# Pooled attention and a two-layer mixer on one core: one group of scores one slot later, two transposes swapped, fifteen idle products instead of sixteen

## The chip, the core and the metric

The kernel runs on one core of a Trainium2 chip. The core has a matrix engine (TensorE, PE in the profile, with its weight loads shown as PEld), a vector engine (VectorE, DVE), an activation engine (ScalarE, ACT), a general engine (GpSimd, POOL) and a queue engine that issues transfers (SyncE, SP); ACT and POOL issue transfers as well. Each engine takes its instructions in a fixed order and waits at semaphores for the others. The metric is the time of one execution on the device in microseconds (us), the median of several runs.

## The reference

Batch 8, 8 heads, 576 tokens, head size 64. Keys and values are averaged over 8 neighbouring tokens, so that each head has 72 of them.

```python
k_p = k.reshape(B, H, Sp, pool, D).mean(axis=3)
v_p = v.reshape(B, H, Sp, pool, D).mean(axis=3)
scores = scale * np.matmul(q, k_p.transpose(0, 1, 3, 2))
scores = scores - np.max(scores, axis=-1, keepdims=True)
attn = np.exp(scores)
attn = attn / (np.sum(attn, axis=-1, keepdims=True) + 1e-09)
attn_out = np.matmul(attn, v_p).astype(np.float32)
...
x = np.ascontiguousarray(attn_out.transpose(0, 2, 1, 3)).reshape(B, S, H * D)
a1 = alpha1 * x + beta1
tok = np.einsum('ts,bsd->btd', w_tok, a1)
u = x + lam * tok
a2 = alpha2 * u + beta2
ch = np.maximum(a2 @ w_ch1, 0.0) @ w_ch2
return (u + lam * ch).astype(np.float32)
```

So there are three stages for each batch: attention over the pooled keys, a mix over the tokens (`w_tok`, 576 x 576), and a two-layer network over the channels (512 to 2048 to 512).

## The kernel before

**Chunks and blocks.** The tokens of a batch are held as four chunks of 128 rows and a rest of 64; the rests of two batches make one more chunk, called (b, 4) by the even batch. Four chunks make a block of 512 rows, and there are nine blocks, n = 0 to 8. The channel network runs block by block. Chunks go in the order (0,0) to (0,3), (1,0) to (1,3), (0,4), (2,0) and so on, so that the second block (n = 1) is the four chunks of batch 1, and its fourth chunk is (1,3).

**The order is written by hand.** Everything ahead of the first block stands in a string of names (from L1116), where each name advances one small generator. From then on, each block n builds a list of pairs (slot, action), sorts it by slot and runs it: that order is the program order on all engines at once, and each engine keeps its own instructions in it. A slot is one unit of matrix work of the block. In block n also the attention of batch n + 1 is done (`attention(b)`, b = n + 1), along with the loads for batch n + 2. The lines of the actions that matter here:

- `mlp_A` (L930, activation L938): one hidden slice j of 16, four products of 128x512 into a bank of the pool psA, then a ReLU by ACT. In block 0, slices 12 to 15 stand in slots 12 to 15.
- `mlp_B` (L951): four products of the second layer for chunk m; `finish_B` (L960, L961) adds the result to the output on DVE in block 0 and issues the store (L970) on SP.
- `att_S4` (L740 for the main rows, L747 for the last 64 rows): the scores of four heads. They take two banks of the pool psB ("lo"), two of psA ("hi") and two more of psA for the last 64 rows ("r"). Six exponentials (L769, ACT) read them: first the two r banks, then pair after pair of the others.
- `att_AV` (L784, L788, then DVE L791 and L793): attention times values of one head, and the division. `att_X` (L807, L800) multiplies two heads' result by a vector into xs, on POOL or DVE; `mix_T` (L873, then DVE L880 and a cast on ACT, L884) is the token mix of a chunk.
- `mix_uT` (L893): transposes a mixed chunk into u_fm, the moving operand of `mlp_A` of its block; from the second block on it is a transposing transfer issued by SP. `att_F` (L586) does the same for the q rows of a batch (qT), and `att_Frem` (L612) for its last 64 rows (rem_qT), which `cast_rem` (L351) has cast on POOL.
- `keep_warm` (L862): products on a tile of zeros that no one reads, ahead of the first real work; two more are issued by "wa" in the string.
- `scale_w2` (L982): multiplies a piece of the second layer's weights by lam, on DVE or POOL; `sum_k` (L360, L362, POOL) sums neighbouring key rows; `att_V` (L692, DVE) does so for values.

Pool psA has six banks and psB two. A bank is handed out again once its last tile's readers, in program order, have been issued; the first instruction that writes it waits for them.

In block 0, with b = 1, the scores of heads 0 to 3 stand in slot 9.0 and those of heads 4 to 7 in slot 12.9; the exponentials, the AVs of heads 4 to 7 and their att_X stand at fixed distances behind them. The transposes of chunks (1,0) to (1,3) stand in slots 23.8, 24.9, 26.0 and 27.1, the one of (0,4) in 28.2, and `att_Frem(2)` in 26.22.

Of the kernel before, what the change touches and what calls it, by code (L numbers as in the profile page):

```python
# [210 lines left out]
def kernel(  # L211
# [30 lines left out]
    def gp(name):  # L242
        if pair[0]:
            return psB.tile([P, 512], FP, tag="ch", bufs=2, name=name)
        return psA.tile([P, 512], FP, tag="gp", name=name)

    def whole(parts):
        for _ in parts:
            pass
# [13 lines left out]
    def new_batch(b):  # L263
        st1[b] = {"qT": [None] * 2, "ET": [None] * H, "raw": [None] * 2, "q": [None] * 2,
                  "k": [None] * 2, "v": [None] * 2}
# [192 lines left out]
    def which_part():  # L458

        one = identity_bf[0:12, 0:12]  # L460
        four = const.tile([12, 4], FP, tag="four", name="four")
        nc.vector.tensor_reduce(out=four, in_=one.rearrange("p (k c) -> p c k", c=4), op=ALU.add,
                                axis=AX.X)
        nc.vector.tensor_copy(out=pick, in_=four.unsqueeze(2).to_broadcast((12, 4, P)))
        for i in range(2):
            nc.vector.tensor_reduce(out=less[:, i:i + 1], in_=one[:, 4 + 4 * i:], op=ALU.add,
                                    axis=AX.X)
        nc.vector.tensor_scalar(out=less, in0=less, scalar1=-1.0, scalar2=None, op0=ALU.mult)
# [108 lines left out]
    def att_F(b, hp, copy=nc.scalar.copy):  # L577


        st = st1[b]  # L580
        u, r = hp // 2, hp % 2
        if st["qT"][u] is None:
            st["qT"][u] = work.tile([P, 8, P], BF, tag="qT", bufs=4, name="qT")
        if b > 1:
            if r == 0:
                nc.sync.dma_start_transpose(out=st["qT"][u],  # L586
                                            in_=st["q"][u].rearrange("p h c d -> p (h c d)"))
            return
        ps_q = gp("ps_q").bitcast(BF)
        for c in range(4):  # L590
            nc.tensor.transpose(
                out=ps_q[:, 128 * c:128 * c + 128],
                in_=st["q"][u][:, 2 * r + c // 2, 2 * (c % 2):2 * (c % 2) + 2].rearrange(
                    "p c d -> p (c d)"),
                identity=identity_bf)

        yield
        copy(out=st["qT"][u][:, 4 * r:4 * r + 4, :],
             in_=ps_q[:, 0:512].rearrange("p (c t) -> p c t", c=4))

    def att_Frem(b, copy=None):

        st = st1[b]
        if b > 2:
            rem = room()[:, 2048:2560].rearrange("p (c t) -> p c t", c=4)
            st["rem_qT"], st["rem_kT"] = rem[:, 0:2], rem[:, 2:4]
            nc.sync.dma_start_transpose(out=rem,
                                        in_=st["rem_both"].rearrange("p c h d -> p (c h d)"))
            return
        st["rem_qT"] = work.tile([P, 2, P], BF, tag="rem_qT", bufs=2, name="rem_qT")  # L610
        if copy is None:
            nc.sync.dma_start_transpose(out=st["rem_qT"],  # L612
                                        in_=st["rem"][0].rearrange("p c h d -> p (c h d)"))
            return
        ps_q = gp("ps_qr").bitcast(BF)
        for c in range(2):
            nc.tensor.transpose(out=ps_q[:, 128 * c:128 * c + 128],
                                in_=st["rem"][0][:, c].rearrange("p h d -> p (h d)"),
                                identity=identity_bf)
        yield  # L620
        copy(out=st["rem_qT"], in_=ps_q[:, 0:256].rearrange("p (c t) -> p c t", c=2))
# [8 lines left out]
    def room():  # L630
        if "room" not in late:
            late["room"] = const.tile([P, 2560], BF, tag="wt_bf", name="late_room")
        return late["room"]
# [224 lines left out]
    def keep_warm(count, ps=None):  # L858

        ps = ps or psB.tile([P, DM], FP, tag="ch", bufs=2, name="ps_warm")  # L860
        for _ in range(count):
            nc.tensor.matmul(out=ps, lhsT=warm[:, 0:P], rhs=warm)  # L862
        return ps
# [202 lines left out]


    new_batch(1)
    warmed = keep_warm(16)
    which_part()  # L1070
    more_constants()

# [56 lines left out]
    def attention(b):  # L1129


        first = b == 1
        todo = []
        if first:
            for hp in range(4):
                todo.append((2.6 + 0.9 * hp, lambda hp=hp: whole(att_F(b, hp))))
            todo.append((3.5, lambda: cast_rem(b, nc.gpsimd, behind=nc.vector)))
            for u in range(2):
                todo.append((3.65 + 0.1 * u, lambda u=u: load_w2(2 + u)))
            todo.append((7.4, lambda: whole(att_Frem(b, nc.scalar.copy))))  # L1140
        if b < B - 1:
            at = 28.5 if first else 10.0
            todo.append((at, lambda: whole(att_F(b + 1, 0))))
            todo.append((at + 0.1, lambda: whole(att_F(b + 1, 2))))
            todo.append((19.3 if first else 23.1, lambda: cast_rem(
                b + 1, nc.gpsimd, behind=None if first else nc.vector)))
            todo.append((26.72 if b > 1 else 26.22, lambda: whole(att_Frem(b + 1))))
        for u in range(2):
            if first:
                todo.append((3.6 + 0.1 * u, lambda u=u: sum_k(b, u, nc.gpsimd)))  # L1150
            if 1 < b < B - 1:
                todo.append((26.5 + 0.1 * u, lambda u=u: sum_k(b + 1, u, nc.gpsimd)))
                todo.append((26.73 + 0.1 * u, lambda u=u: turn_k(b + 1, u)))
            if b > 2:
                todo.append((4.1 + 2.0 * u, lambda u=u: pool_k(b, u)))
                continue
            if first:
                todo.append((19.1 + 0.1 * u, lambda u=u: sum_k(2, u, nc.gpsimd)))
            todo.append((7.0 + 2.3 * u if first else 2.9 + 2.0 * u,
                         lambda u=u: whole(  # L1160
                             att_K(b, u, nc.vector.tensor_copy if first else nc.scalar.copy))))
        for u in range(2):
            at = (9.0, 12.9)[u] if first else (6.3, 13.6)[u]
            todo.append((at, lambda u=u: att_S4(b, u)))
            for k, dt in enumerate((0.1, 0.1, 0.1, 0.7, 1.7, 1.75) if u else (0.1, 0.1, 0.1, 1.1, 2.1, 3.1)):
                todo.append((at + dt, lambda u=u, k=k: st1[b]["exp", u](k)))
            early = (5.2, 5.7, 3.7, 4.2) if first else (5.7, 6.2, 2.9, 3.4)
            for i, dt in enumerate((2.9, 3.4, 4.6, 5.1) if u else early):
                h = 4 * u + i
                todo.append((at + dt, lambda h=h: whole(att_AV(b, h))))  # L1170
                if i % 2:
                    eng = nc.gpsimd if h == 5 or first and h < 5 else nc.vector
                    todo.append((at + dt + 0.1, lambda h=h, eng=eng: att_X(b, h - 1, h + 1, eng)))
        for u in range(2):
            when = (0.2, 1.4, 2.2), (10.0, 12.8, 13.0) if b == 2 else (5.0, 7.2, 8.0)
            if first:
                when = (10.6, 10.7, 10.8), (12.5, 12.6, 12.7)
            for i, at in enumerate(when[u]):
                todo.append((at, lambda u=u, i=i: att_V(b, u, 4 >> i)))
        for c in range(5):  # L1180
            at = 22.0 + 1.1 * c if first else 21.0 + (1.3 if b == 2 else 1.15) * c
            if c < 4 or b % 2:
                todo.append((at, lambda c=c: whole(mix_T(b, c))))
                key = (b, c) if c < 4 else (b - 1, 4)
                todo.append((at + 1.8, lambda key=key: whole(mix_uT(key))))
        return todo

    for n in range(NBLK):
        todo = []
        for j in range(0 if n else 4, NJ):  # L1190
# [3 lines left out]
            else:  # L1194
                at = 8 * (j // 4 % 2) + 4 * (j // 8) + j % 4 if n >= FIRST else j
                todo.append((at, lambda j=j: whole(mlp_A(n, j))))
        for m in range(4 if n < FIRST else 0):
            for part in range(4):
                at = 16 + (4 * part + m if n == 0 else 2 * part + (m if m < 2 else 6 + m))
# [56 lines left out]
        b = n + 1  # L1256
        if b < B:
            todo += attention(b)
            if b + 1 < B:
                new_batch(b + 1)  # L1260
                gate = nc.vector if b == 1 else None
                for u in range(2):
                    at = (15.31 if b == 1 else 21.0) + 0.01 * u
                    todo.append((at, lambda b=b, u=u: load_k(b + 1, u, gate)))
                    at = {1: 14.0, 2: 6.5}.get(b, 0.4) + 0.1 * u
                    todo.append((at, lambda b=b, u=u: load_q_bf(
                        b + 1, u, nc.vector if b == 2 else None)))
                    at = 15.35 + 0.01 * u if b == 1 else ((6.7, 13.2) if b == 2 else (3.5, 7.5))[u]
# [42 lines left out]
```

## Time and profile before

| | us |
|---|---|
| median of three runs | 330.04 (329.70 to 330.65) |
| the profiled execution | 331.23 |
| its span, first to last instruction | 329.4 |
| PE busy | 320.9 |
| DVE, ACT, POOL busy | 236.0, 175.6, 115.8 |
| first idle products to first transposes (PE) | 1.51 to 8.09 |
| first block of the channel network, from its first slice on PE to the start of the second block | 25.15 to 67.55 |
| second block | 67.55 to 102.88 |

The span is what lies between the first and the last instruction; the execution's time has some 1.8 us around it. The granted clock of PE is 1.00 throughout. A row of the timeline gives start, duration, engine, line, operation and the tiles written and read; in brackets at its end stands the idle time ahead of it on its engine, and the instruction whose end the profile holds to have released it. SPq and POOLq rows are the issue of a transfer, not the transfer itself.

### The profile page before, as it was taken

To read this page: it belongs to the slowest core of one execution; us is meant where nothing else is said; L and a number is where in the kernel's file an instruction comes from. 1 tells how busy PE (TensorE), PEld (TensorE's weight loads), DVE (VectorE), ACT (ScalarE), POOL (GpSimd) and SP (SyncE) were. 2 spreads that over 40 slices of the span, in tenths; PEclk is the share of its full clock that TensorE was granted. 3 is DMA by queue.
4 is the path that set the end of the run, shared out by engine and by line. 5 is a ranking of instruction groups with operands and counts; after the bars stand their busy time and mean duration, and the time that the engine had idled before them with its cause. 6 is when DMAs were issued, how large, how long until landed. Compare 5 with 4: busy or idle time off the path is not lost.

```text
span 329.4 us, 6466 instructions
## 1 busy us (share of the span) xinstructions
PE 320.9 (97%) x2473; PEld 206.4 (63%) x2473; DVE 236.0 (72%) x494; ACT 175.6 (53%) x326; POOL 115.8 (35%) x140
## 2 busy tenths in 40 slices
PE   8999989999999999999999999999999999999995
PEld 3689644445544576656775577558755866586584
DVE  6783576996689979786967787887788793263263
ACT  3868979258433951387128803782368235803710
POOL 8687354996246010800280027102510560000000
PEclk9999999999999999999999999999999999999999
DMA  7999979988896893499549943996480025003013
GB/s 197 204 231 254 214 149 265 142 165 170 174 254 103 211 191 90 75 265 178 155 87 242 188 147 81 164 230 180 100 178 0 2 54 158 0 2 127 0 34 96
DMA packets 73351, 47.40 MB, mean 144 GB/s; under 512 B 41283, under 2 KB 64099, under 8 KB 73319
## 3 DMA queue, kind: packets, MB, share of 16 engines
q1 hardware_dynamic: 59302, 34.78, 45.7%
q0 software_dynamic: 12896, 11.28, 21.5%
q10 hardware_dynamic: 1120, 0.92, 0.9%
q8 instruction: 19, 0.31, 0.4%
q14 instruction: 14, 0.11, 0.1%
HBM read 38.31 MB, written 9.44 MB: 145 GB/s over the span
## 4 chain that ended last, share of the span: by engine, by line
PE 82%; DMA 5%; DVE 4%; POOL 3%; issue 3%; ACT 1%; POOLq 0%; SPq 0%; DVEq 0%; ACTq 0%
PE ps_h L930 34%; PE ps_w L1047 23%; PE ps_tok L873 10%; PE ps_ch L951 7%; DMA v<-in_v_dram 2%; DMA kT<-k_bf 2%; PE ps_s L740 2%; PE ps_av L784 2%; ACT H L938 1%; POOL k_bf L362 1%; DVE x_tm L793 1%; POOL k_raw L360 1%; DVE w L982 1%; PE ps_r L747 1%; PE ps_w L516 1%
## 5 line engine op out<-in xcount | busy, mean ns | idle before, releaser
L930 PE MATMUL ps_h<-u_fm,w 128*128 128x512 bf16 (+2 forms) x608 | 132.8, 369 | 2.0 <-DVE u_sb L961 0.8
L938 ACT ACTIVATE H<-ps_h,bias_cols 128x512 bf16<-128x512 f32 x144 | 98.3, 689 | 56.8 <-PE ps_h L930 55.4
L930 PEld LDWEIGHTS <-w 128*128 128x128 bf16 x608 | 65.7, 114 | 53.0 <-issue 4.4
L1047 PEld LDWEIGHTS <-H 128*128 128x128 bf16 x560 | 53.5, 98 | 10.8 <-DVE u_sb L1065 1.2
L884 ACT CAST u_bf<-u_sb 128x512 bf16<-128x512 f32 x34 | 21.1, 619 | 71.3 <-issue 41.4
L1047 PE MATMUL ps_w<-w,H 128*128 128x256 bf16 x448 | 53.6, 273 | 0.0
L807 POOL TENSOR_TENSOR xs<-x_tm,lamal_bc 128x512 bf16<-128x512 f32 x12 | 15.2, 1270 | 104.2 <-DVE x_tm L793 104.0
L1065 DVE TENSOR_TENSOR u_sb<-u_sb,ps_w 128x512 f32<-128x512 f32 x54 | 36.3, 684 | 17.5 <-PE ps_w L1047 17.0
L873 PE MATMUL ps_tok<-xs,wtT 128*128 128x512 bf16 (+5 forms) x220 | 45.1, 361 | 0.0
L880 DVE TENSOR_TENSOR u_sb<-x_tm,ps_tok 128x512 f32<-128x512 f32 (+1 forms) x40 | 27.2, 683 | 8.9 <-PE ps_tok L873 8.9
L793 DVE TENSOR_TENSOR x_tm<-ps_av,recs 128x320 f32<-128x320 f32 x64 | 31.4, 491 | 2.7
L769 ACT ACTIVATE ET<-ps_s 72x512 f16<-72x512 f32 x56 | 32.3, 593 | 0.0
L951 PE MATMUL ps_ch<-w,H 128*128 128x512 bf16 x128 | 30.4, 379 | 0.0
L873 PEld LDWEIGHTS <-wtT 128*128 128x128 bf16 (+3 forms) x220 | 19.2, 100 | 15.2 <-issue 1.1
L791 DVE RECIPROCAL recs<-ps_av 128x5 f32<-128x5 f32 x64 | 12.0, 188 | 18.3 <-PE ps_av L788 18.0
L692 DVE TENSOR_TENSOR v_u<-v_u 72x1024 f32<-72x1024 f32 (+1 forms) x24 | 24.5, 1021 | 0.2
L1047 PE MATMUL ps_w<-w_t,h_s 128*128 128x256 bf16 x168 | 22.6, 272 | 0.0
L360 POOL TENSOR_TENSOR k_raw<-k_raw 128x512 f32<-128x512 f32 x14 | 19.2, 1369 | 4.5 <-DMA k_raw<-in_k_dram 4.5
L951 PEld LDWEIGHTS <-H 128*128 128x128 bf16 x128 | 11.9, 98 | 13.7 <-issue 0.4
L362 POOL TENSOR_TENSOR k_bf<-k_raw 128x512 bf16<-128x512 f32 x14 | 19.1, 1366 | 1.1
L1016 DVE TENSOR_TENSOR h_s<-H 128x1024 bf16<-128x1024 bf16 x21 | 14.6, 696 | 6.3 <-ACT H L938 5.8
L1047 PEld LDWEIGHTS <-h_s 128*128 128x128 bf16 x168 | 16.4, 98 | 4.1
(161 smaller groups left out, 349.8 us busy)
## 6 DMA issues: line engine op xcount, KB each, us to landing
out_dram<-u_sb SPq DMA_DIRECT2D x29, 256.0 KB, 4.1
k_raw<-in_k_dram SPq DMA_DIRECT2D x13, 512.0 KB, 5.7
v_u<-in_v_dram SPq DMA_DIRECT2D x12, 512.0 KB, 5.8
q_bf<-in_q_dram POOLq DMA_DIRECT2D x15, 256.0 KB, 5.6
w<-in_moe_w_ch_dram POOLq DMA_DIRECT2D x6, 512.0 KB, 14.0
out_dram<-u_sb SPq DMA_DIRECT2D x11, 128.0 KB, 2.4
v<-in_v_dram POOLq DMA_DIRECT2D x4, 288.0 KB, 10.4
w<-in_moe_w_ch_dram POOLq DMA_DIRECT2D x1, 1024.0 KB, 14.1
```

Of the source, the lines that this page charges most:

```text
L360: eng.tensor_tensor(out=raw[:, :, 0:2], in0=raw[:, :, 0:2], in1=raw[:, :, 2:4], op=ALU.add)
L362: eng.tensor_tensor(out=bf, in0=twice[0], in1=twice[1], op=ALU.add)
L692: nc.vector.tensor_tensor(out=out, in0=source[:, :, 0:width], in1=source[:, :, width:2 * width], op=ALU.add)
L769: nc.scalar.activation(out=o, in_=i, func=AF.Exp, bias=0.0, scale=0.125 if b < 3 else 0.125 * 0.125)
L793: nc.vector.tensor_tensor(out=x[:, 1 - odd:6 - odd, dd:dd + D], in0=av[:, :, 0:64], in1=rec.unsqueeze(2).to_broadcast((P, 5, D)), op=ALU.mult)
L873: nc.tensor.matmul(out=ps_tok[p0:p1, cols], lhsT=wtT[0:kk, at, P * c:P * c + p1 - p0], rhs=xs_pool[i][0:kk, sc, cols], start=(sc == 0), st ...
L880: nc.vector.tensor_tensor(out=s["u"][p0:p1, :], in0=x[p0:p1, 1 + c if c < 4 else 5 - 5 * i, :], in1=ps_tok[p0:p1, 0:DM], op=ALU.add)
L930: nc.tensor.matmul(out=ps_h[:, t0:t1 + one], lhsT=w1_of(cc, j), rhs=rhs, start=(cc == 0), stop=(cc == 3))
L938: nc.scalar.activation(out=H4[n, j // 4][:, j % 4, :], in_=ps_h, func=AF.Relu, bias=bias_cols[:, j:j + 1], scale=1.0)
L951: nc.tensor.matmul(out=ps, lhsT=H_of(n, j)[:, 128 * m:128 * m + 128], rhs=w2[j // 4][:, j % 4, :], start=(j == 0), stop=(j == NJ - 1))
L1047: nc.tensor.matmul(out=ps, lhsT=stat(j), rhs=moving(j), stop=(j == 7), start=(first and (pp == 0 or alone) and j == 0), skip_group_check=True)
L1065: nc.vector.tensor_tensor(out=o, in0=o, in1=banks[key, "both"], op=ALU.add)
```

## The change

Three numbers change.

```diff
     new_batch(1)
-    warmed = keep_warm(16)
+    warmed = keep_warm(15)
     which_part()
...
-            todo.append((26.72 if b > 1 else 26.22, lambda: whole(att_Frem(b + 1))))
+            todo.append((26.72 if b > 1 else 27.2, lambda: whole(att_Frem(b + 1))))
...
         for u in range(2):
-            at = (9.0, 12.9)[u] if first else (6.3, 13.6)[u]
+            at = (9.0 if first else 6.3, 13.6)[u]
             todo.append((at, lambda u=u: att_S4(b, u)))
             for k, dt in enumerate((0.1, 0.1, 0.1, 0.7, 1.7, 1.75) if u else (0.1, 0.1, 0.1, 1.1, 2.1, 3.1)):
                 todo.append((at + dt, lambda u=u, k=k: st1[b]["exp", u](k)))
```

Sorted by slot, block 0 then has these sequences (all else keeps its place):

```
before: slice 12, AV 2, scores 4-7, slice 13, exp 0 1 2, AV 3, X 2-3, exp 3, slice 14, AV 0, exp 4 5, AV 1, X 0-1, slice 15, loads,
        AV 4, B0, AV 5, X 4-5, B1, AV 6, B2, AV 7, X 6-7, B3
after:  slice 12, AV 2, slice 13, AV 3, X 2-3, scores 4-7, exp 0 1 2, slice 14, AV 0, exp 3, AV 1, X 0-1, slice 15, exp 4, loads (exp 5 among them),
        B0, AV 4, B1, AV 5, X 4-5, B2, AV 6, AV 7, X 6-7, B3
...
before: transpose (1,2), q rows of batch 2 (last 64), mix (0,4), B2, transpose (1,3), B0, finish, transpose (0,4), qT of batch 2
after:  transpose (1,2), mix (0,4), B2, transpose (1,3), q rows of batch 2 (last 64), B0, finish, transpose (0,4), qT of batch 2
```

Here "exp" are the exponentials of heads 4 to 7, B0 to B3 the second layer's products of chunks 0 to 3, and "loads" those for batch 2. In the other batches nothing changes: the two slots for b > 1 are the same in both versions.

## The prediction

> **What bounds the kernel now.** I read part 1 of the page first, then the list of waits over the whole span.
>
> ```profile
> span 329.4 us, 6466 instructions
> PE 320.9 (97%) x2473; PEld 206.4 (63%) x2473; DVE 236.0 (72%) x494; ACT 175.6 (53%) x326; POOL 115.8 (35%) x140
> ```
> ```profile
> PE ps_warm L862 <- DVE early L402: 1.5, 1, 1.5
> PE ps_s L740 <- ACT ET L769: 0.9, 1, 0.9
> PE ps_h L930 <- DVE u_sb L961: 0.8, 1, 0.8
> PE ps_h L930 <- ACT H L938: 0.6, 1, 0.6
> PE ps_sc L702 <- ACT kp L671: 0.5, 1, 0.5
> ```
> TensorE (PE) is idle for 8.5 us, of which 3.35 us lie behind its last work (326.05 to 329.4) and 1.5 us ahead of its first. So the kernel is a list of matmuls with few holes, and only a hole that closes, without another opening, makes it shorter. The 0.9, the 0.6 and the 0.8 lie in or right behind the first block, where the change works. The timelines of these places, all engines, come next (columns: start, duration).
>
> ```profile
> 40.49 0.28 PE L784 MATMUL ps_av<-vp,ET 72*128 72x66 f16 x4
> 40.73 0.30 PE L740 MATMUL ps_s<-qT,kp 64*72 64x256 bf16 x1
> 41.34 0.58 ACT L769 ACTIVATE ET<-ps_s 72x512 f16<-72x512 f32 x1
> 41.97 0.27 PE L740 MATMUL ps_s<-qT,kp 64*72 64x256 bf16 x1 [0.94 <-ACT ET L769]
> 42.37 0.49 DVE L793 TENSOR_TENSOR x_tm<-ps_av,recs 128x320 f32<-128x320 f32 x1
> 42.66 1.06 PE L930 MATMUL ps_h<-u_fm,w 128*128 128x512 bf16 x4
> 43.75 0.69 ACT L938 ACTIVATE H<-ps_h,bias_cols 128x512 bf16<-128x512 f32 x1 [1.83 <-PE ps_h L930]
> 44.49 1.03 PE L930 MATMUL ps_h<-u_fm,w 128*128 128x512 bf16 x4 [0.62 <-ACT H L938]
> ```
> ```profile
> 61.02 0.62 ACT L884 CAST u_bf<-u_sb 128x512 bf16<-128x512 f32 x1 [1.32 <-DVE u_sb L880]
> 63.69 1.17 SPq L612 DMA_TRANSPOSE rem_qT<-rem_q  x1
> 64.95 1.22 SPq L893 DMA_TRANSPOSE u_fm<-u_bf  x1
> 66.80 0.69 DVE L961 TENSOR_TENSOR u_sb<-u_sb,ps_ch 128x512 f32<-128x512 f32 x1
> 67.55 0.81 PE L930 MATMUL ps_h<-u_fm,w 128*128 128x512 bf16 x3 [0.80 <-DVE u_sb L961]
> ```
> In the first, the scores of heads 4 to 7 begin at 40.73, and their second product waits until 41.97 for the last exponential of heads 0 to 3 (ends 41.92), whose bank it takes. Hidden slice 13 follows at 42.66, AV of head 3, and slice 14 at 44.49, behind the ReLU of slice 13 (43.75 + 0.69 = 44.44). That fits buffers that come round in the order in which they were given back: of the six in psA the scores take four (two for main, two for the last 64 rows), slice 13 and AV 3 get the other two, slice 14 gets slice 13's. In the second, SyncE (SP) stands at the third batch's q rows until 63.69, when POOL has cast them (62.81 + 0.86); behind it stands the transpose of the second block's fourth chunk, whose cast was done at 61.64. The second block starts at 67.55.
>
> **Part 1, scores one slot later.** New order on PE: slice 12, AV 2, slice 13, AV 3, scores, slice 14, AV 0, AV 1, slice 15, and then each AV of heads 4 to 7 one product later. No instruction is added. Slice 13 (0.87 us by starts) and AV 3 (0.15) now run from 40.73 to 41.75; slice 13 gets the buffer of slice 10, read long ago. Main products of the scores go on at 41.97, as before. But the buffers come out otherwise: the second rest buffer is now AV 2's, which DVE reads until 42.37 + 0.49 = 42.86. With 0.05 us from release to start (44.44 to 44.49) that product starts at 42.91, and the 0.58 us that lay behind it (42.08 to 42.66) end the scores at 43.49. Slice 14 takes slice 13's buffer: its ReLU, no longer behind the stall, ends near 42.63. So slice 14 starts at 43.49 instead of 44.49: **1.00 us won**. No row shows the new wait. If another buffer came up it would fall away (scores end 42.66, 1.83 won); if it also waited for the DVE instruction behind it (42.78 + 0.41 = 43.19), 0.67 are left. I take 1.00, since the free order explains both 43.55 and 44.49.
>
> The Trainium skill, Perfetto Trace Analysis (Tensor Engine Instruction), says that a matmul's end in a profile is estimated, not observed; the row at 42.66 agrees, lasting 1.06 us where slice and AV give the next start 0.89 later. By the idle figures, which use such ends, the two parts would win at most 0.94 + 0.62 + 0.80 less the new wait of 0.81, or 1.55 us; I go by starts.
>
> What is late next: exponentials 4 and 5 now stand behind the ReLU of slice 15 (PE 44.66 to 45.53, ReLU to 46.35) and end at 47.4; AV 6 needs them at 48.44. AV 6 and 7 come close together, so the DVE product into xs ends near 51.8 against 52.2 for the mix. POOL's X of heads 2 and 3 goes from 44.71 to about 44.0, and with it the two q loads issued behind it (46.46) and its last X, which ends at 51.4. ACT's weight scalings start at 47.4, not 47.70. All of it stays hidden; where the cover went, each us late would cost one.
>
> **Part 2, the q rows' transpose behind the chunk's.** The same two DMA issues, swapped on SP. The chunk's cast is ready at 61.64, some 1.0 earlier with part 1. Its own 1.22 us issue goes into the time in which SP stood waiting for POOL, so the q rows still go out at 63.69 or earlier, and the stores, the chunk of rows 512 to 575 and batch 2's qT behind them lose nothing. The page puts PE's wait on a DVE row that ends at 67.49; but the tile that hidden slice 0 of block 1 needs is u_fm. DMA rates in 0.15 us slices show the chunk's data moving at 66.15 to 66.9, and other transposes land about 0.6 us behind their data (issue 59.72 + 4.5 = 64.2, data to 63.6), so 67.5 fits the transpose too. Slice 0's psA buffer is that of a mix which DVE finished with at 59.0 or before. I take the transpose. Issued at 60.7, it lands by 65.2 even with the 4.5 us of the one before it. PE's twenty products at 62.26 take 20 x 0.2157 (3.45 us for 16, by starts 49.74 to 53.19), to 66.58: the hole is **0.97 us**, and it goes. Bounds: 0 if DVE is the releaser, 0.97 if not.
>
> **Part 3, fifteen idle products.** Eighteen (two more by "wa") run from 1.51 to 8.09; starts are 0.427 us apart at first, 0.21 in the end, so one less frees 0.21. The real transposes can take it (their first cast ends near 7.28). But PE waits at 13.95:
> ```profile
> 13.95 0.80 PEld L680 LDWEIGHTS <-identity_bf 72*72 72x72 bf16 x8 [0.35 <-DMA v<-in_v_dram]
> ```
> That v transfer was issued by POOL at 5.82 and does not hang on PE. So 0; 0.21 won if ACT or DVE behind 13.95 gain by the earlier start. A loss is excluded: nothing reads the product, and PE stays busy until real work is ready.
>
> **Sum.** 1.00 + 0.97 + 0 = 1.97 us. Block 1 would start at 65.6. What it meets there: slice 4 of block 1 (71.18, then 69.21) takes the buffer that DVE's last L961 frees at 69.45 + 0.69 = 70.14, or 69.19 if DVE moves by 1.0, just in time. S4 of batch 2 (74.05, then 72.1) needs qT: issue 68.22 + 4.5 = 72.7, or 71.7 moved. From 67.5 to 240 PE has 0.3 us of holes, so the gain should last. The profiled execution, 331.23 (span 329.4 and 1.83 around it), lies 1.19 above the median 330.04. I apply the difference to the median: **328.1 us**, 327.5 to 328.8 by the bounds above.
>
> **Rivals.**
> 1. DVE does not move in time. L982 took 0.68 us alone at 55.08, and 2.50 for two at 60.91 while POOL's rows at 59.47 and 61.26 ran. If POOL stays where it is (k arriving at 56.5 regardless), DVE leaves those two at the same 63.4, and L961 ends at 70.14: slice 4 goes from 71.18 to 70.19, 0.99 won, 329.05 us. For it: the DMA share is 1.16 at 50 to 63, full. Against: the gates of those loads (47.01) stand behind AV 1, which moves 1.0, and the share is only 0.33 at 45.3 to 49. The Trainium skill, SBUF — State Buffer (SBUF: two separate sides), has DVE and GpSimd hold a shared port pair as an exclusive lock; by that rule the stretched DVE rows end with POOL's, which is this rival. Chance 0.14.
> 2. The page is right, and DVE's L961 releases block 1. Then only DVE's 1.0 counts: 329.0 us. Against it: the buffers above. Chance 0.08.
> 3. Lost later. The chain of waits goes through kT transposes, DVE and then PE at 185.69 without slack. If loads, not PE, pace that chain, all is given back: 330.0. For it: DMA 91% busy in 67.5 to 103. Against: POOL's casts wait there on DVE (27.8 us in 4 waits), and DVE on PE. Chance 0.12.
> 4. Slower: kT transposes fall beside loads. At 172.03 one took 7.04 us, at 101 the landing took 4.7. Should the shifted loads stretch two more of the later pairs by the 2.34 between, at places with no slack as at 185.69, 4.7 us are lost: 330.04 - 1.97 + 4.7 = 332.8. It decides from 2.0 us of such lateness on. For it: that edge; against: all queues shift by nearly the same. Chance 0.10.
>
> **How the numbers follow.** The forecast has 0.56. The range 327.5 to 329.7 takes in rivals 1 and 2 and leaves out 3 and 4, 0.22 less what of 3 ends below 329.7. 0.3% is 0.99 us, about what a measurement tells from no change. Faster: 0.56 and half of rivals 1 and 2, which lie on that bound: 0.67. Same: the other half and rival 3, 0.23. Slower: 0.10.
>
> **What would show it.** Right: no wait of L740 for the exponential near 41; a product of L747 held until a DVE L793 ends near 42.9; slice 14 near 43.5; on SP the u_fm issue near 60.7, then the q rows; block 1 at 65.6 with no hole ahead of it; the v wait still at 13.95. Wrong: block 1 releasing right behind an L961 (rival 2), a hole near 69 to 70 (rival 1), L740 rows waiting for qT near 72, or a block 2 that does not start before 102.88, as it does now (rival 3).

## The result, and the profile after

The changed kernel takes 328.08 us (median of five, 327.80 to 328.87), the kernel before 329.74 us in as many runs beside it. The ratio is 0.9947, with a 95% interval of 0.9929 to 0.9965: between 1.2 and 2.3 us faster. A few executions of several versions, the kernel before among them, take 2 to 7 us more at a lower granted clock; the ratios leave the slowest out, and the others widen some intervals.

Part 1 of the page after:

```profile
span 326.2 us, 6464 instructions
PE 319.8 (98%) x2472; PEld 206.2 (63%) x2472; DVE 235.5 (72%) x494; ACT 175.8 (54%) x326; POOL 116.0 (36%) x140
```

That span is 3.2 us below the one of the first profile, about twice what the medians show. So one of the two profiled executions is not a typical one, and it was the first, as the experiments will show. The longest waits of PE in the list after:

```profile
PE ps_warm L862 <- DVE early L402: 1.5, 1, 1.5
PE ps_v L680 <- DMA v<-in_v_dram: 0.5, 1, 0.5
PE ps_sc L702 <- ACT kp L671: 0.5, 1, 0.5
PE ps_h L930 <- ACT u_fm L905: 0.4, 1, 0.4
```

The three waits in and right behind the first block are gone, and one has come: 0.5 us for v, at 13.85. Next the timeline at the scores after the change (start, duration; rows in between are left out, here and below):

```profile
40.52 1.04 PE L930 MATMUL ps_h<-u_fm,w 128*128 128x512 bf16 x4
41.22 0.58 ACT L769 ACTIVATE ET<-ps_s 72x512 f16<-72x512 f32 x1
41.65 0.47 PE L740 MATMUL ps_s<-qT,kp 64*72 64x256 bf16 x2
41.70 0.68 ACT L938 ACTIVATE H<-ps_h,bias_cols 128x512 bf16<-128x512 f32 x1
42.03 0.66 PE L740 MATMUL ps_s<-qT,kp 64*72 64x256 bf16 x3
42.26 0.49 DVE L793 TENSOR_TENSOR x_tm<-ps_av,recs 128x320 f32<-128x320 f32 x1
42.43 0.26 PE L747 MATMUL ps_r<-rem_qT,kp 64*72 64x64 bf16 x1
42.82 1.06 PE L930 MATMUL ps_h<-u_fm,w 128*128 128x512 bf16 x4
```

Slice 13 now runs ahead of the end of the last exponential of heads 0 to 3 (41.22 + 0.58 = 41.80), which frees a bank for the scores. The three main products at 42.03 are drawn as lasting 0.66 us where three without a stop take 0.38: one of them waits, until slice 13's ReLU ends at 41.70 + 0.68 = 42.38, and the next rest product (L747, the last 64 rows) starts at 42.43. No idle figure shows this stop. (The Trainium skill, Perfetto Trace Analysis, Tensor Engine Instruction, has a matmul's end as an estimate; here it hides a stop that the starts show.) Slice 14 starts at 42.82, 0.07 behind DVE's read of AV 2 (42.26 + 0.49 = 42.75). From slice 12's start to slice 14's it took 39.62 to 44.49 before, 4.87 us, and 39.50 to 42.82 now, 3.32: 1.55 us less.

The second place, after the change:

```profile
55.71 5.57 SPq L893 DMA_TRANSPOSE u_fm<-u_bf  x4
60.61 4.49 PE L951 MATMUL ps_ch<-w,H 128*128 128x512 bf16 x20
61.37 1.20 SPq L612 DMA_TRANSPOSE rem_qT<-rem_q  x1
64.69 0.69 DVE L961 TENSOR_TENSOR u_sb<-u_sb,ps_ch 128x512 f32<-128x512 f32 x1
64.94 2.75 PE L930 MATMUL ps_h<-u_fm,w 128*128 128x512 bf16 x12
```

All four chunk transposes go out in a row, the q rows behind them. Block 1 (the second block; block 0 is the first) starts at 64.94, right behind the twenty products, and before the L961 that the first page held for its releaser has ended (65.38). It starts 2.61 us earlier than in the first profile, blocks 2, 3 and 4 do so by 2.62, 2.61 and 2.62, and block 5 by 3.20.

### The profile page after: what moved, and what is told of

Read it like the earlier page. It is cut to its first block, busy times and chain, and to the rows that moved or that the text cites. A ratio compares the mean times of both kernels' runs of the same rounds, so it can differ in the third digit from the quotient of the medians.

```text
span 326.2 us, 6464 instructions
## 1 busy us (share of the span) xinstructions
PE 319.8 (98%) x2472; PEld 206.2 (63%) x2472; DVE 235.5 (72%) x494; ACT 175.8 (54%) x326; POOL 116.0 (36%) x140
## 4 chain that ended last, share of the span: by engine, by line
PE 93%; DMA 2%; ACT 2%; POOL 1%; issue 0%; DVE 0%; POOLq 0%; ACTq 0%
PE ps_h L930 38%; PE ps_w L1047 26%; PE ps_tok L873 12%; PE ps_ch L951 9%; DMA v<-in_v_dram 2%; PE ps_s L740 2%; PE ps_av L784 2%; ACT H L938 1%; PE ps_r L747 1%; PE ps_av L788 1%; PE ps_w L516 1%; ACT ET L769 0%; PE ps_rs L529 0%; ACT u_fm L905 0%; POOL v L308 0%; PE ps_v L680 0%
## 5 line engine op out<-in xcount | busy, mean ns | idle before, releaser
L807 POOL TENSOR_TENSOR xs<-x_tm,lamal_bc 128x512 bf16<-128x512 f32 x12 | 15.3, 1271 | 102.6 <-DVE x_tm L793 102.3
```

## The experiments

Each was timed beside the kernel before on the same chip. The ratios are to that kernel.

| | what | median us | ratio (95%) |
|---|---|---|---|
| e1 | scores alone | 328.46 | 0.9957 (0.9944 to 0.9971) |
| e2 | q rows alone | 329.71 | 0.9999 (0.9991 to 1.0008) |
| e3 | fifteen idle products alone | 329.94 | 1.0028 (0.9998 to 1.0059) |
| e4 | scores and q rows | 328.30 | 0.9957 (0.9944 to 0.9970) |
| e5 | before, keys late | 336.12 | 1.0178 (1.0130 to 1.0226) |
| e6 | before, keys late, q rows moved | 334.11 | 1.0132 (1.0074 to 1.0190) |
| e7 | before once more | 329.81 | one run |
| e8 | full change, scores at 13.1 | 328.15 | 0.9944 (0.9910 to 0.9977) |
| e9 | full change, four idle products | 334.67 | 1.0127 (1.0101 to 1.0152) |
| e10 | full change, AV 2 read earlier | 329.46 | 0.9972 (0.9937 to 1.0008) |
| e11 | full change once more | 328.26 | 0.9953 (0.9939 to 0.9967) |
| e12 | e10 once more | 327.93 | 0.9939 (0.9910 to 0.9967) |

**e1, the scores alone.** The kernel before with one line:

```diff
-            at = (9.0, 12.9)[u] if first else (6.3, 13.6)[u]
+            at = (9.0 if first else 6.3, 13.6)[u]
```

> Only the scores of heads 4 to 7 go to slot 13.6; the q rows' transpose stays at 26.22 and sixteen idle products run. Theory A (the two holes interact): hidden slice 14 starts near 42.8 instead of 44.5, and everything behind it, POOL's cast of the q rows too, comes so much earlier (60.8 instead of 63.7) that the q rows no longer hold up the chunk's transpose: it goes out near 62.0, lands near 64.6, and block 1 starts near 65.0 with no hole. The whole gain then comes from this part alone, as much as the full change, 1.7 us (0.995). Theory B (they add up): the q rows still hold the chunk's transpose, the hole of 0.97 us ahead of block 1 stays, block 1 starts near 66.0, and the gain is some 1.0 us less than that of the full change.

Theory A holds. Slice 14 starts at 43.13 (slice 13 at 40.84, 2.29 us, as in the full change), the q rows go out at 61.10 and the chunk's transpose at 62.36, and block 1 starts at 65.25 without a hole. The time is that of the full change within both intervals.

**e2, the q rows alone.**

```diff
-            todo.append((26.72 if b > 1 else 26.22, lambda: whole(att_Frem(b + 1))))
+            todo.append((26.72 if b > 1 else 27.2, lambda: whole(att_Frem(b + 1))))
```

> Only the q rows' transpose goes to slot 27.2. Theory A and B alike: the hole of the scores stays (slice 14 near 44.5), the chunk's transpose goes out near 61.7, the hole of 0.97 us ahead of block 1 is gone, block 1 starts near 66.6, and the gain is near 1.0 us (0.997). Rival, by the page: DVE's L961 (ends 67.49) releases block 1, which then still starts at 67.5, and nothing is won (1.000).

Half of this failed. Block 1 starts at 66.59 with no hole, as the theory said, and yet nothing is won against the median of the kernel before. So either the gain is lost later, or the typical execution of the kernel before has no such hole. e7 decides.

**e3, fifteen idle products alone.**

```diff
-    warmed = keep_warm(16)
+    warmed = keep_warm(15)
```

> Only the number of idle products goes from 16 to 15. Theory: the real transposes start some 0.2 us earlier (more if the matrix engine's early slow phase ends at another moment), the wait for the v transfer near 13.9 grows by the same, and nothing is won (1.000 within 0.1%). Rival: engines behind that wait had been late by the early phase, and 0.2 us are won (0.9994).

Nothing is won. Its trace was worth more than its time: neither the scores nor the q rows are moved in it, and block 1 starts at 66.48, without the hole. On the other hand block 4 took 35.75 us there (169.69 to 205.44), against 34.58 in e2 and in the full change; a slice and a product of the scores wait for DVE:

```profile
182.82 1.05 PE L930 MATMUL ps_h<-u_fm,w 128*128 128x512 bf16 x4 [0.28 <-DVE x_tm L793]
184.59 0.30 PE L740 MATMUL ps_s<-qT,kp 64*72 64x256 bf16 x1 [0.20 <-DVE x_tm L793]
```

The two waits come to 0.48 us, but by starts the stretch from the AVs ahead of them to the next slice takes 1.17 us more than in e2 (182.07 to 185.22, against 182.17 to 184.15), which is all that block 4 lost. DVE is late there because the second turned key tile is: it is pooled at 178.61, in e2 at 177.46, though both kernels issue the two transposes within 0.1 us of each other (169.66 and 169.76).

**e4, both moves, sixteen idle products.** The two lines of e1 and e2 together.

> The scores and the q rows' transpose both moved, with sixteen idle products as before: the full change without its third part. Theory: the same as the full change, 0.995, block 1 near 65.0. Rival: the fifteenth product counts, and this is 0.2 us or more behind the full change.

As expected: 0.9957, block 1 at 65.29. The third part of the change is worth nothing that shows here.

**e7, the kernel before once more, for its trace.**

> The kernel before once more, for its trace. Theory (after the traces of e2 and e3): the hole ahead of block 1 in the first profile came from keys that landed late in that execution (56.5, 5.7 us from issue to landing); usually they land near 55.5, SP is free by 62.3, block 1 starts near 66.5 with no hole, and the q rows' slot is worth nothing. Rival: the hole of 0.97 us is there in every execution (block 1 near 67.5).

The theory holds. Its rows, POOL, SP and PE:

```profile
55.73 1.34 POOL L360 TENSOR_TENSOR k_raw<-k_raw 128x512 f32<-128x512 f32 x1 [3.45 <-DMA k_raw<-in_k_dram]
62.61 1.17 SPq L612 DMA_TRANSPOSE rem_qT<-rem_q  x1
63.87 1.22 SPq L893 DMA_TRANSPOSE u_fm<-u_bf  x1
66.76 2.75 PE L930 MATMUL ps_h<-u_fm,w 128*128 128x512 bf16 x12
```

The chunk's transpose is still held up by the q rows (its cast is done at 61.90), but at 63.87 it is early enough. Slice 14 to block 1 takes 22.10 us here, 23.06 in the first profile and 22.12 after the change. The keys took 4.9 us from issue to landing here and 4.5 to 5.0 in e1 to e4 and after, but 5.7 in the first profile and 5.5 in e8 and e9; why it varies stays open. Block 4 takes 34.57 here, 35.16 there. So the first profile had 0.96 and 0.59 us of its own, 1.55 in all; its span without them, 327.85, is close to the 328.0 of e7.

**e5 and e6, the late keys made on purpose.** If lateness of the keys makes the hole, more of it makes a bigger one, and the q rows' slot then counts.

```diff
-                    at = (15.31 if b == 1 else 21.0) + 0.01 * u
+                    at = (15.37 if b == 1 else 21.0) + 0.01 * u
                     todo.append((at, lambda b=b, u=u: load_k(b + 1, u, gate)))
```

> The kernel before, with the loads of batch 2's keys issued behind those of its values instead of ahead of them (slot 15.37 for 15.31). Nothing else is changed; q rows' transpose at 26.22. The keys then land some 5 us later (near 60.5; 1.15 MB of values at some 220 GB/s lie ahead), POOL sums them and casts the q rows near 67.3 instead of 62 to 64. Theory (SP, standing at the q rows, holds the chunk's transpose): the chunk's transpose goes out near 68.6, block 1 starts near 71.2 with a hole of more than 4 us ahead of it, and the kernel takes 4 us more than before (1.012 to 1.014). Rival, by the page's row of the kernel before: DVE's L961 releases block 1; DVE does not wait for the q rows, so block 1 starts near 67.5 at the latest and little is lost (under 1.004).

e6 has the line of e2 as well.

> The same late keys, and the q rows' transpose at 27.2. Theory: the chunk's transpose goes out near 61.7, block 1 starts near 66.6 without a hole, and of the 4 us and more that the late keys cost alone, at least half comes back; what stays is a wait of some 2 us for batch 2's qT, which stands behind the q rows on SP, at its scores near 73 to 75 (1.004 to 1.008). Rival (DVE releases block 1): no difference to the late keys alone, within 0.3%.

The mechanism shows to 0.1 us. First e5, then e6:

```profile
67.41 1.17 SPq L612 DMA_TRANSPOSE rem_qT<-rem_q  x1
68.67 1.22 SPq L893 DMA_TRANSPOSE u_fm<-u_bf  x1
71.27 4.92 PE L930 MATMUL ps_h<-u_fm,w 128*128 128x512 bf16 x12 [4.44 <-issue]
```
```profile
66.68 2.75 PE L930 MATMUL ps_h<-u_fm,w 128*128 128x512 bf16 x12
67.44 1.17 SPq L612 DMA_TRANSPOSE rem_qT<-rem_q  x1
83.34 0.30 PE L740 MATMUL ps_s<-qT,kp 64*72 64x256 bf16 x1 [1.72 <-DVE x_tm L793]
```

With the same late cast (67.4 in both) block 1 starts 4.6 us apart, only by the order of two issues on SP. The rival that DVE releases block 1 falls. The prices were off: e5 lost 6.25 us, not 4, since the matrix engine came out of the hole slow (below), and in e6 2.0 of them came back by the medians of four executions each, a third rather than half; one of e6's four, 336.32, took as long as those of e5. In e6 the qT wait was 0.29 us. A hole of 1.72 us came later in the block, behind a DVE read, and slow products followed it (below). That read was late because two multiplications ahead of it on DVE were long: L807 and L800 took 1.69 and 1.24 us (at 78.67 and 80.28) while POOL's weight scalings (L982) still ran, until 83.67. In e7, where those end at 77.68, the two take 0.69 and 0.28 us (at 78.39 and 79.00). That POOL's work stretches DVE's is argued from these rows; no run separates it.

**e8, the scores one place earlier.** The full change with the scores behind slice 13, but ahead of AV 3.

```diff
-            at = (9.0 if first else 6.3, 13.6)[u]
+            at = (9.0, 13.1)[u] if first else (6.3, 13.6)[u]
```

> The full change, but the scores of heads 4 to 7 in slot 13.1: behind hidden slice 13 and ahead of AV 3. By the banks that the program assigns, no product of the scores then waits for the ReLU of slice 13; slice 14 still takes AV 2's bank, which DVE reads until about 42.75. Theory (DVE's read of AV 2 is what holds slice 14): the scores end near 42.6 without a wait, and slice 14 still starts near 42.8, so the time is that of the full change (0.995). Rival (the ReLU wait inside the scores is what costs): slice 14 starts up to 0.4 us earlier, and the time falls by as much against the full change.

The theory holds. The scores run through after the last exponential (rests at 42.03, 42.14, 42.35 and 42.44), with no stop for the ReLU, and slice 14 starts 2.28 us behind slice 13, as in the full change (2.30). That start, 42.98, lies 0.06 behind the end of DVE's read of AV 2 (42.43 + 0.49 = 42.92), so this read is what holds it.

**e9, four idle products.** The full change with `keep_warm(4)` in place of `keep_warm(15)`.

> The full change, but only four idle products (six with the two of "wa") instead of fifteen. Six products 0.427 us apart end near 4.1; the real transposes need the first cast of q, near 7.3, so the matrix engine stands idle for 3 us and then goes on, up to 0.25 us earlier than in the full change. Theory (the idle products matter only through the early slow phase, in which starts are twice as far apart): the real work from 7.3 on runs in that phase, the wait for v near 13.9 is used up and 1 to 3 us are lost (1.000 to 1.004 against before, 0.3 to 0.9% behind the full change). Rival (the wait for v covers it all): the same as the full change (0.995).

The direction is that of the theory, the size well beyond it: 6.4 us behind the full change (334.67 to 328.26 on the same chip). The timeline of e9, then the same v products after the change:

```profile
7.34 1.13 PE L591 MATMUL ps_q<-identity_bf,q_bf 128*128 128x128 bf16 x8 [3.08 <-ACT q_bf L288]
16.25 1.92 PE L680 MATMUL ps_v<-v,identity_bf 72*72 72x256 f16 x8
24.76 2.23 PE L873 MATMUL ps_tok<-xs,wtT 128*128 128x256 bf16 x10
```
```profile
13.85 1.06 PE L680 MATMUL ps_v<-v,identity_bf 72*72 72x256 f16 x8 [0.51 <-DMA v<-in_v_dram]
```

Eight products take 1.92 us in place of 1.06. The ten mix products at 24.76 are still slow (2.07 us to the next start, where the chain before has 1.10), so the slow phase lasts from 7.34 to about 26.5, and the v transfer, the cover of the prediction, is passed by 2.4 us. The first slice starts at 31.95, after the change at 25.04. Whether the smaller number of idle products or the 3.08 us of idle behind them keeps the engine slow isn't separated here.

**e10 and e12, DVE's read of AV 2 moved.** What e8 found is removed: DVE reads AV 2 ahead of the second sum of values. With that the program also exchanges two banks: the scores now get AV 2's, and slice 14 slice 13's.

```diff
-                when = (10.6, 10.7, 10.8), (12.5, 12.6, 12.7)
+                when = (10.6, 10.7, 10.8), (12.5, 12.75, 12.8)
```

> The full change, and DVE reads AV 2 one instruction earlier: the second and third sum of batch 1's values (heads 4 to 7) go from slots 12.6 and 12.7 to 12.75 and 12.8, behind AV 2. Theory: DVE's read of AV 2 ends near 42.1 instead of 42.75, the scores then wait for nothing after the last exponential, slice 14 starts near 42.55 instead of 42.8, and 0.2 us more are won, which the trace can show and the median hardly can (0.994). Rival: the sums' delay passes on to AV 3's read and from there to slice 15's bank, and the 0.2 us are given back there.

e10's profiled execution had a granted clock of about 0.5 from 12 to 24 us. Behind 26 us it is 1.00 again, and there slice 14 starts 2.01 us behind slice 13 (45.91 to 47.92) and block 1 24.15 us behind it (70.06). e12 is the same kernel, traced without the slow stretch.

> The kernel of e10 once more, since the matrix engine's clock was low from 11.6 to 24 us in e10's profiled execution, ahead of the place in question. Theory: from the start of slice 13 to that of slice 14 it takes 2.05 us instead of 2.30 (full change) and block 1 starts 0.2 us earlier against slice 13; the time is 0.994 to 0.995, not to be told from the full change. Rival: slice 15 waits for AV 3's read instead, and slice 13 to block 1 takes as long as in the full change.

```profile
41.84 0.49 DVE L793 TENSOR_TENSOR x_tm<-ps_av,recs 128x320 f32<-128x320 f32 x1
42.84 1.06 PE L930 MATMUL ps_h<-u_fm,w 128*128 128x512 bf16 x4
```

Slice 13 starts at 40.83, slice 14 2.01 us later instead of 2.30, and slice 13 to block 1 takes 24.15 us against 24.42 after the change, 24.41 in e8 and 24.41 in e11. So 0.26 us are won and kept, by the traces of e10 and e12 alike. The two ends that matter now come in time: the read at 42.33 for the scores, slice 13's ReLU at 42.68 for slice 14. The times (0.9939 with an interval of 0.9910 to 0.9967 in e12) can't tell the win from the full change.

**e11, the full change once more.**

> The full change once more, beside the others on one chip. Theory: 0.995 again; slice 14 near 42.8, block 1 near 65.0, no hole ahead of it, and the differences between its executions come from transfers that land at other times.

0.9953; slice 14 at 43.05, 2.29 behind slice 13, block 1 at 65.17. The full change thus repeats.

## Why the prediction was right, and where it was not

The time was met: 328.1 predicted, 328.08 measured, a gain of 1.97 forecast and 1.66 measured between the medians. That the time agrees to 0.02 us is luck. Two of its terms were wrong by over half a us, with opposite signs (1.00 for 1.55, 0.97 for 0), and the sum was taken from a median of 330.04, while the kernel before took 329.74 beside the changed one. Nor do the ends 327.5 and 328.8 follow from the bounds of the terms: those give a win of 0.67 at the least and of 3.01 at the most, 329.4 and 327.0 us.

**Part 1, the scores: right mechanism, too small.** Put at 1.00, it measures 1.55 (4.87 to 3.32 us from slice 12 to slice 14; e7 and e11 have 4.88 and 3.32), and carries the whole change (e1). The step that failed is the bank: the prediction had banks come round in the order in which they were given back, and so let a rest product of the scores wait for DVE's read of AV 2 until 42.91. The built program gives a main product of the scores slice 13's own bank there, whose ReLU ends at 42.38, and gives AV 2's bank to slice 14, which waits for it until 42.82. The order had been read out of two starts (43.55 and 44.49) that other orders explain as well. Its upper bound, 1.83, was the nearer one. e8 and e12 show which of the two waits sets slice 14: the DVE read. Of the 0.48 us of standstill that slice 13 to 14 still has (2.30 against some 0.87 + 0.15 + 0.80 of work for slice 13, AV 3 and the scores, by starts of the first profile), e12 removes 0.29.

**Part 2, the q rows: right mechanism, worth nothing in the medians.** Put at 0.97, it measures 0 (e2: 0.9999, 0.9991 to 1.0008). That SP stood at the q rows, and that the page's releaser was not the real one, is shown (after, e5, e6). What failed is that the hole was taken for a fixed part of the kernel: it was in the one execution that was profiled, where the keys landed about 1 us late, and not in e3 or e7. The sum was made against a profile 1.19 us above the median, and where that difference lay was not asked; this hole (0.96) and the one in block 4 (0.59) make it up and more, and a hole that the median doesn't have can't be won from it. There is a second reason: with part 1 the q rows themselves come 2.9 us earlier than in the first profile (63.69 to 60.8), so that they held up nothing in e1's trace, with keys that took 4.5 us. With late keys part 2 would still count. In e8 they took 5.5 us, and the q rows went out at 62.48. In the old order the chunk's transpose would have followed 1.26 us later, as in the first profile, and block 1 2.60 us behind that, as in the first profile and in e5: at 66.3 instead of 65.11. This is an estimate from those rows; no run times it.

**Part 3, the idle product: right.** The transposes started earlier (7.55 for 8.09; the idle products themselves had become fast sooner) and the wait for v grew to 0.51 us. e3 and e4 show no gain.

**What it meets later.** No hole in block 1: slice 4 and qT were in time, as worked out. Rival 1 (DVE stays) did not come: its last L961 ends at 68.03, 2.1 us earlier. Rival 2 falls by the order of 64.94 and 65.38, and by e5 and e6. Rival 3 (lost later) falls, since blocks 2 to 4 keep 2.6 us. Rival 4 named a real thing, but not of the change: turned keys that land late cost block 4 0.59 us in the first profile and 1.17 in e3, both with the scores unmoved; none of the six traces with the scores moved, e9 and e10 left aside, shows it at block 4, and e2 and e7, with the scores unmoved, don't either. Whether that is chance is open.

## What to carry to other kernels

Before a hole of a profile goes into a sum, ask how far that execution lies from the median, and whether what ends the hole is a transfer whose landing varies; a second trace of the same kernel would have shown 0.97 us to be nothing. Where an instruction is moved across takers of a shared pool of banks, its new waits come from the bank that it is given, and that is read from the program's assignment and not guessed from two starts. Two issues on one queue are worth putting in the order in which their inputs come, even where it gains nothing: with the inputs late the wrong order put block 1 4.6 us back, and by the medians it cost the kernel 2 us.

## What the runs showed of the hardware

**A hole can cost more than its length.** In e5, behind 4.44 us of idle, twelve products took 4.75 us by starts (71.27 to 76.02) and not 2.59. Three stretches, of e5, e6 and e10; the third figure from the end is PE's granted clock:

```profile
71.20:76.00 4.80, 4.74 (x12) 1.71 (x13) 3.12 (x7) 1.38 (x2) 4.80 (x4) 0.53 0.81 198
```
```profile
86.00:87.00 1.00, 1.00 (x4) 0.39 (x3) 0.06 (x2) 0.71 (x3) 0.00 (x0) 0.50 1.30 174
```
```profile
12.00:13.00 1.00, 1.00 (x21) 1.00 (x19) 0.97 (x2) 0.91 (x3) 0.34 (x1) 0.50 1.18 208
```

The Trainium skill, TensorE: Matmul & The Clock Gate (What's actually happening), has the clock fall to half after an idle window of some 3.4 us and come back after as much sustained work; e5 agrees, with 0.53 over 4.8 us. e6 and e10 differ. In e6 a hole of 1.72 us, which ended at 83.34, was followed by half clock from 86 to 88 (0.50). In e10 the clock stood at 0.50 from 12 to 24 us, and ahead of that no hole of PE between 1.51 and 12 us is above 0.45 us. Here the measurement decides: in this kernel the clock can halve without an idle window of that length. That the hole of 1.72 us was the cause in e6 isn't shown. In none of the traces after the change, e1, e4, e8, e11 or e12, does a wait of PE behind 25 us exceed 0.4 us.

**The slow phase need not show in the clock's row.** In e9 the granted clock stands at 1.00 in all stretches from 0 to 33 us, while products take nearly twice as long until about 26.5 (1.92 us for 1.06); only the durations tell.
